# Order of work at the head, at chunks' ends and before the experts in a fused attention and MoE kernel

## The chip, the core and the metric

The kernel runs on one core of a Trainium2 chip. TensorE (PE) multiplies matrices; VectorE (DVE), ScalarE (ACT) and GpSimd (POOL) work on tiles in on-chip memory; SyncE (SP) issues most of the transfers (DMAs). The metric is the time of one execution on the device in microseconds (us). Of the kernel before there are three runs and one profiled execution.

## What is computed

```python
scores = (1 / S) * z @ z.T                  # B = 8, S = 2496, z: S x 64
out = (maximum(scores, 0) ** 2) @ v         # v: S x 256
x = (u * out).reshape(B * S, 256)
logits = x @ w_gate                         # 8 experts
# per token: its best expert, weight = softmax(logits)[best] = gate_w
# per expert e: of its tokens the 80 with the largest gate_w
h = maximum(x[tok_idx] @ w1[e], 0)          # 256 -> 1024
result[tok_idx] = gate_w[tok_idx] * (h @ w2[e])   # all other rows are 0
```

All values are 32-bit floats.

## The kernel before

**Precision.** PE multiplies in a reduced 32-bit format. Each operand is split into a high part (a cast to that format) and a low part (the value less the high part), and three products replace one: high by high, high by low and low by high. So z gives `zs` or `zm`, v gives `vt`, and the attention weights `a` give `ah` and `al`. High parts are casts, on ACT mostly; low parts are subtractions on DVE (helper `tt`, L55).

**Tiles.** A chunk is a batch and 512 of its queries: 8 x 5 = 40 chunks (`at(n)`), each with ten pairs of 128-key tiles. For one pair: scores on PE into two PSUM tiles `s` (`begin`, L399); ACT's Relu (L402) and Square (L405) into `a`; the cast to `ah` on ACT (L408) or, in the chunk's own diagonal blocks, on DVE (L413) (all three in `middle`); `al` on DVE (`low`); then the accumulation on PE into two banks `acc` (`attend_half`, L544), in two groups per pair. The scores are symmetric, so most blocks are computed once: DVE transposes `a` (`turn`, L304), SP writes it to DRAM (`y`) and reads it back as `blk` (L358), where ACT casts it (`mirrored`, L376) and DVE subtracts.

**Loops.** The first chunk's first five steps run in one lane (`for t in range(HALF)`, HALF = 5). Then two chunks run side by side (`for t in range(HALF, END)`): step t handles the entries e and e + 1, while the pairs e + 3 and e + 4 are prepared. Every fifth step ends a chunk: `chunk_x_first` (DVE, `xf`, L569) multiplies u into accumulator bank 0, `chunk_x_copy` (ACT, L584) copies bank 1, and both banks are free for the next chunk only then. Chunks with an even number end in the middle of a step, those with an odd number at its end. In between stand steps for the next batch (`z_and_v`): a load of 512 columns of z (`load_z`, 256 KB), its split (`prep_zs`, L121 and L55), loads and splits of v (`prep_v`, cast L108, low part L159). The last chunk runs in one lane again, beside the logits of the chunk before it (`chunk_logits`, PE L684, from the parts `xb` that `chunk_hi` and `chunk_lo` make).

**What sets the order.** PE, ACT, DVE and SP work in the order in which the program is written (a manual schedule), each engine in its own queue; semaphores hold an instruction until what it reads is there. POOL does the same in the last stage. SP has up to eight DMAs under way: a further one is issued when an older one, whose semaphore it uses again, has landed.

**Head.** A tile `idle` is set to zero on POOL (L181); nine matmuls on it (`warm`, L186) run until z has arrived. Then come the scores of the first two pairs, the whole of v's first tile, and the third pair's scores ahead of the first accumulation. Between the first accumulating matmuls two more `warm` stand.

**Experts.** Behind the attention the experts' tokens are found (`token`, on DVE), their rows are gathered from DRAM by POOL (`xg`, L1589), copied (`xf`, L110), turned by PE (`ffn_x`, `xp`, L1621) and put through two layers (`ffn1`, `ffn2`). The last chunk's gate values are made by DVE (`gate_near`, `gate_sum`: L744 to `gall`, L758), turned by PE (`gt`, L769), copied (`gs`) and written to DRAM (`gate_store`, `gd`, L772), from where `target` gathers them. SP loads the experts' weights (`wraw`, L861).

## Time and profile before

| | us |
|---|---|
| runs before | 1351.98, 1353.8, 1354.32 (median 1353.8) |
| profiled execution, in all | 1355.23 |
| its span, first to last instruction | 1353.3 |
| PE busy | 1329.6 (98%) |
| DVE busy | 1085.8 (80%) |
| ACT busy | 1020.1 (75%) |
| POOL busy | 40.1 (3%) |

The mean granted clock of PE in the profiled execution is 0.993 of full speed. PE's matmuls on 64 rows come in twos that run at the same time in two halves of the array, so "a pair of matmuls" is two rows of the trace. In a timeline a bracket shows how long an engine sat idle before an instruction and who released it. In the list of waits each row has the waiting engine and its tile and line, the one waited for, the sum in us, how many times, and the longest.

### The profile page before, as it was taken

How to read it: one execution, taken by the hardware profiler on the slowest of the kernel's cores; microseconds unless marked ns; L12 is line 12 of the kernel's file. 1: busy time of each engine (PE TensorE's matmuls, PEld its weight loads, DVE VectorE, ACT ScalarE, POOL GpSimd, SP SyncE). 2: the span in 40 equal slices, each digit the busy share in tenths (PEclk: the TensorE clock that was granted, in tenths of full speed). 3: DMA queues.
4: the chain of work that ended last, by engine and by line, in shares of the span. 5: the costliest groups of instructions: out<-in, count | busy, mean ns of one | idle time of the engine just before them, and what ended most of it. 6: DMA issues, size and time to landing. Idle time of an engine off the chain costs nothing.

```text
span 1353.3 us, 32346 instructions
## 1 busy us (share of the span) xinstructions
PE 1329.6 (98%) x12887; PEld 1210.7 (89%) x12887; DVE 1085.8 (80%) x1667; ACT 1020.1 (75%) x1361; POOL 40.1 (3%) x42
## 2 busy tenths in 40 slices
PE   8999999999999999999999999999999999999997
PEld 5789998999899997999889998999889998898776
DVE  6777888887887888878878888878888778777886
ACT  6776787677867787776877778776877678777666
POOL 0000000000000000000000000000000000000065
PEclk8999999999999999999999999999999999999999
DMA  5799989999899998999899998999979997989945
GB/s 164 223 269 258 283 224 289 241 277 244 259 239 250 290 262 227 270 247 261 222 262 269 257 285 225 260 264 261 249 237 243 286 267 214 290 226 274 272 136 188
DMA packets 286013, 337.12 MB, mean 249 GB/s; under 512 B 96824, under 2 KB 206368, under 8 KB 275616
## 3 DMA queue, kind: packets, MB, share of 16 engines
q1 hardware_dynamic: 284832, 333.68, 93.8%
q8 instruction: 103, 1.69, 0.5%
q0 software_dynamic: 1024, 1.31, 0.3%
q14 instruction: 54, 0.44, 0.1%
HBM read 162.67 MB, written 135.48 MB: 220 GB/s over the span
## 4 chain that ended last, share of the span: by engine, by line
PE 83%; DVE 6%; ACT 4%; DMA 4%; issue 2%; SPq 0%; POOL 0%; DVEq 0%; POOLq 0%; ACTq 0%
PE acc L544 69%; PE s L399 9%; PE pl L684 2%; ACT a L402 1%; ACT a L405 1%; DVE al L55 1%; DMA blk<-y 1%; PE s L461 1%; DMA wraw<-w 1%; DVE x L304 1%; DVE vt L159 1%; PE warm L186 0%; ACT xf L584 0%; DMA y<-x 0%; PE op L1699 0%
## 5 line engine op out<-in xcount | busy, mean ns | idle before, releaser
L544 PE MATMUL acc<-ah,vt 64*128 64x512 f32 (+1 forms) x6004 | 845.9, 387 | 6.3 <-DVE xf L569 3.7
L544 PEld LDWEIGHTS acc<-ah,vt 64*128 64x128 f32 x6004 | 660.0, 185 | 60.1 <-DVE xf L569 6.7
L544 PE MATMUL acc<-al,vt 64*128 64x512 f32 (+1 forms) x3002 | 503.9, 389 | 0.4 <-DVE al L55 0.2
L55 DVE TENSOR_TENSOR al<-a,ah 128x1024 fp32r<-128x1024 f32 (+2 forms) x240 | 272.3, 1135 | 174.4 <-ACT ah L408 76.7
L544 PEld LDWEIGHTS acc<-al,vt 64*128 64x128 f32 x3002 | 340.0, 185 | 23.5 <-DVE al L55 1.1
L402 ACT ACTIVATE a<-s 128x512 f32<-128x512 f32 (+1 forms) x408 | 221.0, 594 | 141.7 <-PE s L399 138.8
L376 ACT CAST ah<-blk 128x1024 fp32r<-128x1024 f32 x160 | 167.1, 1047 | 102.7 <-PE acc L544 94.2
L55 DVE TENSOR_TENSOR al<-blk,ah 128x1024 fp32r<-128x1024 f32 x160 | 193.4, 1214 | 38.2 <-PE acc L544 10.7
L405 ACT ACTIVATE a<-a 128x1024 f32<-128x1024 f32 x204 | 216.3, 1060 | 6.3
L304 DVE STREAM_TRANSPOSE x<-a 128x512 f32<-128x512 f32 x320 | 207.6, 687 | 0.0
L408 ACT CAST ah<-a 128x1024 fp32r<-128x1024 f32 x160 | 168.0, 1050 | 5.8 <-PE acc L544 0.8
L399 PE MATMUL s<-zm,zs 64*128 64x512 f32 x960 | 148.7, 392 | 4.1 <-ACT a L402 4.1
L399 PEld LDWEIGHTS s<-zm,zs 64*128 64x128 f32 x960 | 107.2, 185 | 14.3 <-ACT a L402 5.7
L1589 POOL DMA_INDIRECT xg<-xs,tok x8 | 13.0, 1630 | 1294.7 <-ACT w2h L888 1286.1
L159 DVE TENSOR_TENSOR vt<-vraw,vt 128x1024 fp32r<-128x1024 f32 (+1 forms) x40 | 46.3, 1156 | 1.6 <-ACT vt L108 1.3
L55 DVE TENSOR_TENSOR xf<-xf,xb 128x1024 f32<-128x1024 f32 (+1 forms) x38 | 45.2, 1189 | 0.4
L55 DVE TENSOR_TENSOR xb<-xf,xb 128x1024 bf16<-128x1024 f32 (+1 forms) x38 | 45.1, 1186 | 0.2
L108 ACT CAST vt<-vraw 128x1024 fp32r<-128x1024 f32 (+3 forms) x56 | 44.9, 830 | 0.0
L594 ACT CAST xb<-xf 128x1024 bf16<-128x1024 f32 (+1 forms) x39 | 39.8, 1020 | 5.0 <-DVE xf L55 2.8
L602 ACT CAST xb<-xf 128x1024 bf16<-128x1024 f32 (+1 forms) x38 | 38.8, 1020 | 5.4 <-DVE xf L55 5.4
L399 PE MATMUL s<-zm 64*128 64x512 f32 x264 | 42.3, 400 | 0.4 <-ACT a L402 0.4
L413 DVE CAST ah<-a 128x1024 fp32r<-128x1024 f32 (+1 forms) x44 | 29.7, 675 | 14.1 <-ACT a L405 14.1
(190 smaller groups left out, 905.9 us busy)
## 6 DMA issues: line engine op xcount, KB each, us to landing
y<-x SPq DMA_DIRECT2D x80, 1024.0 KB, 6.9
blk<-y SPq DMA_DIRECT2D x320, 256.0 KB, 6.9
out<-idle SPq DMA_DIRECT2D x40, 512.0 KB, 7.8
vraw<-v SPq DMA_DIRECT2D x32, 512.0 KB, 9.3
zm<-zs SPq DMA_DIRECT2D x128, 128.0 KB, 4.8
ut<-uT SPq DMA_DIRECT2D x32, 512.0 KB, 6.8
xs<-xq SPq DMA_DIRECT2D x32, 512.0 KB, 6.6
wraw<-w SPq DMA_DIRECT2D x28, 512.0 KB, 5.3
```

The source lines that it names most:

```text
L55: V.tensor_tensor(out=o, in0=a, in1=b, op=op)
L108: eng.copy(out=o, in_=i)
L159: e1.tensor_tensor(out=vt[:, :nf, 1], in0=raw[:, :nf], in1=vt[:, :nf, 0], op=ALU.subtract)
L304: V.transpose(out=x[:, :, :, t].rearrange("p n k s -> p k n s"), in_=a)
L376: nc.scalar.copy(out=natural(ah), in_=src)
L399: nc.tensor.matmul(s, zk, zm[rows, :, y].rearrange("p h k t -> p k h t"), start=i == 0, stop=i == 2)
L402: nc.scalar.activation(out=a[:, h, :nc_], in_=s[:, :nc_], func=AF.Relu)
L405: nc.scalar.activation(out=a[:, :, :nc_], in_=a[:, :, :nc_], func=AF.Square)
L408: nc.scalar.copy(out=st["ah"][:, :, :nq], in_=a[:, :, :nq])
L544: ins = nc.tensor.matmul(acc[c], vt, mv, start=p == pairs[0] and group == 0 and i == 0, stop=p == pairs[-1] and group == 1 and i == len(mm ...
L594: nc.scalar.copy(out=xb[:, 0], in_=xf)
L602: nc.scalar.copy(out=xb[:, 1], in_=xr)
```

## The change

The kernel after does the same arithmetic on the same tiles; it issues it in another order, splits the first pair's work between two engines, and loads less of z.

- **Head.** The first 128 columns of `idle` are set first and eight warm matmuls read these. `first_pair` computes the first pair's `a` in two halves, one on ACT and one on DVE, with v's first tile loaded and cast in halves between them. The third pair's scores (`begin(2)`) go between the accumulating matmuls, in the place of two warm ones.
- **Single-lane steps.** `middle` loses the cast to `ah`, which becomes a step of its own, `cast`; v's cast stands ahead of it.
- **First two-lane step.** `group(e, 0)` goes ahead of `begin(e + 3)`.
- **Sides of z.** Apart from columns 0 to 511, only those rows and columns are loaded that `zs` uses: two DMAs of 64 KB in pieces of 512 bytes replace one of 256 KB, and two operations on 128 rows replace four on 64.
- **Chunks' ends.** At even ends `chunk_x_first` and `chunk_x_copy` go ahead of `low(e + 3)`; at odd ends ahead of `cast(e + 4)`.
- **z and v.** In `z_and_v` v's split goes ahead of z's.
- **Late steps.** The store and the high and low parts of the chunk before the last are written one entry earlier; a gather into a small unused tile is added on POOL.
- **Experts.** A memset and an empty instruction on POOL stand ahead of the first gather and take its waits for stored rows. The gate values of the last chunk (`gate_near`, `gate_sum`, `gate_store`) go behind the tokens of experts 2 and 3; SP's write of them (`gd`) stands ahead of four weight loads in SP's order, before and after. The sums over counts are spread between the first experts' steps.

```diff
+        if j:
+            raw = raw[:, :CH // 2]
+            load_sides(raw, b, j, j + 1)
+        else:
+            nc.sync.dma_start(out=raw, in_=zT[b, :, :CH])
         return raw
+
+    def load_sides(raw, b, j0, j1):
+
+        for h in range(2):
+            rows = slice(h * HP, (h + 1) * HP)
+            src = zT[b, rows, j0 * CH:j1 * CH].rearrange("p (k h t) -> p k h t", h=2, t=P)
+            nc.sync.dma_start(out=raw[rows].rearrange("p (k t) -> p k t", t=P), in_=src[:, :, h])
...
-        for h in range(2):
-            rows = slice(h * HP, (h + 1) * HP)
-            src = tiles_of(raw)[rows, :, h]
-            V.tensor_copy(out=zs[rows, 0], in_=src)
-            tt(zs[rows, 1], src, zs[rows, 0], ALU.subtract)
+        src = raw.rearrange("p (k t) -> p k t", t=P)
+        V.tensor_copy(out=zs[:, 0], in_=src)
+        tt(zs[:, 1], src, zs[:, 0], ALU.subtract)
...
+            nc.tensor.matmul(wm, idle[:, :P], idle[:, :P].rearrange("p (o t) -> p o t", o=1).broadcast_to([P, QT, P]),
+                             start=True, stop=True)
+
+    warm(8, ps_m, "m")
+    nc.gpsimd.memset(idle[:, P:], 0.0)
...
+    def first_pair(v_high, v_low):
+
+        zm = zm_t[0, 0]
+        a = pair_tile("a", 0, 0, 0, F32, 2)
+        ah = pair_tile("ah", 0, 0, 0, bufs=4)
+        ss = [ps_s.tile([P, CH], F32, tag="s", name=f"s_0_0_{h}") for h in range(2)]
+        for i, (x, y) in enumerate(((0, 0), (1, 0), (0, 1))):
+            for h, s in enumerate(ss):
+                rows = slice(h * HP, (h + 1) * HP)
+                nc.tensor.matmul(s, zm[rows, h, x, 0], zm[rows, :, y].rearrange("p h k t -> p k h t"),
+                                 start=i == 0, stop=i == 2)
+        nc.scalar.activation(out=a[:, 0], in_=ss[0], func=AF.Relu)
+        ts(a[:, 1], ss[1], 0.0, ALU.max)
+        v_high(0)
+        nc.scalar.activation(out=a[:, 0], in_=a[:, 0], func=AF.Square)
+        tt(a[:, 1], a[:, 1], a[:, 1], ALU.mult)
+        nc.scalar.copy(out=ah[:, 0], in_=a[:, 0])
+        V.tensor_copy(out=ah[:, 1], in_=a[:, 1])
+        v_low(0)
+        al = pair_tile("al", 0, 0, 0)
+        tt(al, a, ah, ALU.subtract)
+        a_t[0, 0, 0] = (ah, al)
...
-            if start_up and i == len(ks):
-                warm(2, ps_m, "m")
+            if start_up and i == 2 * len(ks):
+                between()
...
+            vb = b if tm < NP else b + 1
+            if 0 < vb < B and tm in V_SPLIT:
+                g = V_SPLIT[tm]
+                prep_v(vb, g, v_raw.pop((vb, g)), nc.scalar, V)
             if 0 < zb < B:
                 if tm in Z_SPLIT:
                     j = Z_SPLIT[tm]
                     (prep_zs if j else prep_zm)(zb, j, z_raw.pop((zb, j)))
...
         for t in range(HALF):
-            if t == 0:
-                begin(2)
-            group(t, 0)
+            group(t, 0, lambda: begin(2))
             if t:
                 begin(t + 2)
             middle(t + 2)
             first_parts(t)
+            cast(t + 2)
             group(t, 1)
             low(t + 2)
             turn(t + 2)
...
             n_end = t // HALF - 1 if t % HALF == HALF - 1 else None
+            if t == HALF:
+                group(e, 0)
             begin(e + 3)
             middle(e + 3)
-            group(e, 0)
+            cast(e + 3)
+            if t > HALF:
+                group(e, 0)
             finish(t, 0)
             transfers(e)
             group(e + 1, 0)
@@ -1199,18 +1255,22 @@
             if t % HALF == 0:
                 logits(t // HALF - 3, 2)
             group(e, 1)
-            low(e + 3)
             if n_end is not None and n_end % 2 == 0:
                 chunk_x_first(*at(n_end))
                 chunk_x_copy(*at(n_end))
+            low(e + 3)
             turn(e + 3)
             middle(e + 4)
+            second = n_end is not None and n_end % 2 == 1
+            if not second:
+                cast(e + 4)
             finish(t, 1)
             transfers(e + 1)
             group(e + 1, 1)
-            if n_end is not None and n_end % 2 == 1:
+            if second:
                 chunk_x_first(*at(n_end))
                 chunk_x_copy(*at(n_end))
+                cast(e + 4)
             low(e + 4)
...
+                    x = 2 * (i - e) + j
+                    if x == 1:
+                        chunk_store(*at(n))
+                    elif x != NP - 2:
+                        finished(*at(n), x)
+                    if x == 2:
+                        chunk_hi(*at(n))
+                    elif x == NP - 3:
+                        chunk_lo(*at(n))
+                    if x:
+                        finished(*at(n - 1), NP + x)
...
+            xg_t[0] = rows_tile(0)
+            late["stored"].append(nc.gpsimd.memset(xg_t[0][:num(0)], 0))
+            ready = nc.gpsimd.engine_nop()
+            for x in late["stored"]:
+                after(ready, x)
...
             many_pe()
+            many_counts()
+            whole(0)
+            many_products()
+            ffn_x(0)
+            many_fetch((2,))
+            ffn_xl(0)
+            many_rows()
+            many_within()
+            ffn1(0, 0)
+            whole(1)
+            token(2)
+            token(3)
+            ffn_x(1)
             gate_near(B - 1, NQ - 1)
             gate_sum(B - 1, NQ - 1, NQ)
-            whole(0)
-            gate_store(P, NCOL - P, ps_t, "t")
-            ffn_x(0)
-            many_counts()
-            many_fetch((2,))
-            ffn_xl(0)
-            ffn1(0, 0)
-            whole(1)
-            many_rows()
-            many_within()
-            token(2)
-            ffn_x(1)
             ffn_xl(1)
             ffn1(0, 1)
-            token(3)
-            loads(4, PL)
             ffn_h(0, 0)
+            gate_store(P, NCOL - P, ps_t, "t")
+            loads(4, xg_t[3][3])
             many_fetch((4, 6))
             ffn1(1, 0)
             empty()
+            token(4)
             target(0)
             target(1)
-            token(4)
             ffn_h(0, 1)
             whole(2)
             ffn1(1, 1)
             ffn2(0, FIRST_J)
             ffn_x(2)
+            spread(3)
             ffn_xl(2)
             ffn2(0, LAST_J)
             token(5)
@@ -1835,7 +1920,6 @@
             half_lo()
             target(2)
             target(3)
-            spread(3)
```

**ACT at the head.** `a_0_0` is the first pair's weights, `s_` its scores, `vt_0` v's first tile. Before:

```order
L402 ACT_TABLE_LOAD
L402 ACTIVATE a_0_0_154<-s_0_0_155 128x512
L402 ACTIVATE a_0_0_154<-s_0_1_156 128x512
L405 ACTIVATE a_0_0_154<-a_0_0_154 128x1024
L108 CAST vt_0_170<-vraw_0_115 128x4x256
L402 ACTIVATE a_0_2_173<-s_0_2_174 128x512
L402 ACTIVATE a_0_2_173<-s_0_3_175 128x512
L405 ACTIVATE a_0_2_173<-a_0_2_173 128x1024
L402 ACTIVATE a_0_4_206<-s_0_4_207 128x512
L402 ACTIVATE a_0_4_206<-s_0_5_208 128x512
```

After:

```order
L456 ACT_TABLE_LOAD
L456 ACTIVATE a_0_0_156<-s_0_0_158 128x512
L1109 CAST vt_0_149<-vraw_0_116 128x2x256
L459 ACTIVATE a_0_0_156<-a_0_0_156 128x512
L461 CAST ah_0_0_157<-a_0_0_156 128x512
L416 ACTIVATE a_0_2_176<-s_0_2_177 128x512
L416 ACTIVATE a_0_2_176<-s_0_3_178 128x512
L1109 CAST vt_0_149<-vraw_0_116 128x2x256
L419 ACTIVATE a_0_2_176<-a_0_2_176 128x1024
L416 ACTIVATE a_0_4_221<-s_0_4_222 128x512
```

The cast of v's first tile is two halves now, the second behind the next pair's relus, and the first pair's cast to `ah` (on DVE before) stands in part on ACT.

**DVE at the first even chunk's end.** `xf_0` reads accumulator bank 0; `zs_1` is the next batch's z. Before:

```order
L121 CAST zs_1_843<-zraw_585 64x256
L55 TENSOR_TENSOR zs_1_843<-zraw_585,zs_1_843 64x256
L121 CAST zs_1_843<-zraw_585 64x256
L55 TENSOR_TENSOR zs_1_843<-zraw_585,zs_1_843 64x256
L475 CAST ah_1_6_860<-a_1_6_848 128x512
L55 TENSOR_TENSOR al_1_6_897<-a_1_6_848,ah_1_6_860 128x512
L55 TENSOR_TENSOR al_1_6_897<-shared,ah_1_6_860 128x512
L569 SCALAR_TENSOR_TENSOR xf_0_900<-acc_0_0_217,ut_0_602 128x512
L55 TENSOR_TENSOR al_2_2_918<-blk_2_0_649,ah_2_2_904 128x1024
```

After:

```order
L130 CAST zs_1_841<-zraw_581 128x256
L55 TENSOR_TENSOR zs_1_841<-zraw_581,zs_1_841 128x256
L610 SCALAR_TENSOR_TENSOR xf_0_892<-acc_0_0_211,ut_0_599 128x512
L516 CAST ah_1_6_856<-a_1_6_844 128x512
L55 TENSOR_TENSOR al_1_6_897<-a_1_6_844,ah_1_6_856 128x512
L55 TENSOR_TENSOR al_1_6_897<-shared,ah_1_6_856 128x512
L55 TENSOR_TENSOR al_2_2_914<-blk_2_0_646,ah_2_2_900 128x1024
```

`xf` stands right behind z's split, which has two operations instead of four, and ahead of `ah` and the two low parts.

**DVE at the first experts.** `xf` is an expert's gathered rows, `tok` its tokens' numbers, `gall` the last chunk's gate values. Before:

```order
L744 TENSOR_SCALAR fw_4_19253,nsum<-d_4_19249 128x32
L746 SCALAR_TENSOR_TENSOR ex_4_19251<-ex_4_19251,fw_4_19253 128x32
L55 TENSOR_TENSOR s_7_4_19407<-ex_4_19251 128x16
L55 TENSOR_TENSOR s_7_4_19409<-s_7_4_19407 128x8
L55 TENSOR_TENSOR s_7_4_19411<-s_7_4_19409 128x4
L59 TENSOR_SCALAR s_7_4_19411<-s_7_4_19411 128x4
L758 RECIPROCAL gall<-s_7_4_19411 128x4
L110 COPY xf_19415<-xg_19344 80x2x256
L771 COPY gs_19419<-gt_19417 32x128
L1516 TENSOR_REDUCE cnt_all<-scratch 128x6
L55 TENSOR_TENSOR xTl_19433<-xp_19422,xTh_19425 128x160
L110 COPY xf_19444<-xg_19359 80x2x256
```

After:

```order
L121 COPY xf_19405<-xg_19331 80x2x256
L1666 TENSOR_SCALAR lw_19407,j_19408<-ws_19389,rin_all 80x256
L61 TENSOR_SCALAR tok_19410<-j_19408,base_all 80x1
L1666 TENSOR_SCALAR lw_19414,j_19415<-ws_19389,rin_all 80x256
L61 TENSOR_SCALAR tok_19417<-j_19415,base_all 80x1
L784 TENSOR_SCALAR fw_4_19223,nsum<-d_4_19219 128x32
L786 SCALAR_TENSOR_TENSOR ex_4_19221<-ex_4_19221,fw_4_19223 128x32
L55 TENSOR_TENSOR s_7_4_19428<-ex_4_19221 128x16
L55 TENSOR_TENSOR s_7_4_19430<-s_7_4_19428 128x8
L55 TENSOR_TENSOR s_7_4_19432<-s_7_4_19430 128x4
L59 TENSOR_SCALAR s_7_4_19432<-s_7_4_19432 128x4
L798 RECIPROCAL gall<-s_7_4_19432 128x4
```

The chain from `fw` to `gall` stood ahead of the first `xf`; it begins behind the second `xf` and two tokens now.

## Rows read from the trace of the kernel before

**Rows 1.** the page: busy time by engine, the DMA queue, the chain by engine
```profile
PE 1329.6 (98%) x12887; PEld 1210.7 (89%) x12887; DVE 1085.8 (80%) x1667; ACT 1020.1 (75%) x1361; POOL 40.1 (3%) x42
...
q1 hardware_dynamic: 284832, 333.68, 93.8%
...
PE 83%; DVE 6%; ACT 4%; DMA 4%; issue 2%; SPq 0%; POOL 0%; DVEq 0%; POOLq 0%; ACTq 0%
```

**Rows 2.** PE's waits, whole run: who waited for whom, us in total, times, longest
```profile
PE s L399 <- ACT a L402: 4.5, 5, 2.0
PE acc L544 <- DVE xf L569: 3.7, 5, 1.5
...
PE xp L1621 <- DVE xf L110: 1.4, 2, 0.7
PE acc L544 <- DVE vt L159: 1.3, 4, 0.4
PE pl L684 <- DVE xb L55: 1.1, 1, 1.1
```

**Rows 3.** timeline of the first 17 us: start, us, what xcount [idle before <-releaser]
```profile
1.39 4.02 PE L186 MATMUL warm<-idle 128*128 128x512 bf16 x9 [1.39 <-POOL idle L181]
...
7.03 1.08 ACT L402 ACTIVATE a<-s 128x512 f32<-128x512 f32 x2 [4.93 <-PE s L399]
...
7.68 0.96 PE L399 MATMUL s<-zm 64*128 64x512 f32 x5 [0.42 <-ACT a L402]
...
9.11 1.03 ACT L108 CAST vt<-vraw 128x1024 fp32r<-128x1024 f32 x1
...
10.68 1.65 PE L399 MATMUL s<-zm,zs 64*128 64x512 f32 x5 [2.03 <-ACT a L402]
...
11.71 1.48 PE L544 MATMUL acc<-ah,vt 64*128 64x512 f32 x4
```

**Rows 4.** two stretches after that: us, busy (xcount) by engine, PEclk, DMA share, GB/s
```profile
11.70:17.20 5.50, 5.37 (x21) 2.78 (x19) 4.67 (x8) 4.53 (x6) 0.00 (x0) 0.50 0.58 164
17.20:29.00 11.80, 11.80 (x102) 9.47 (x100) 7.25 (x12) 8.19 (x11) 0.00 (x0) 1.00 0.37 130
```

**Rows 5.** the chain of waits, 42 to 51 us: start, us, what
```profile
42.49 7.88 DMA blk<-y
...
50.43 0.04 ACT ah L376
```

**Rows 6.** timeline at the first step of two lanes
```profile
34.72 0.29 DVE L121 CAST zs<-raw 64x256 fp32r<-64x256 f32 x1
35.05 0.42 DVE L55 TENSOR_TENSOR zs<-raw,zs 64x256 fp32r<-64x256 f32 x1
...
35.74 0.96 PE L399 MATMUL s<-zm,zs 64*128 64x512 f32 x5 [1.37 <-ACT a L402]
```

**Rows 7.** timeline at an even and at an odd chunk's end
```profile
70.70 0.68 DVE L569 SCALAR_TENSOR_TENSOR xf<-acc,ut 128x512 f32<-128x512 f32 x1
...
71.43 0.95 PE L544 MATMUL acc<-ah,vt 64*128 64x512 f32 x5 [1.46 <-DVE xf L569]
...
227.62 1.05 ACT L408 CAST ah<-a 128x1024 fp32r<-128x1024 f32 x1
...
228.57 0.59 ACT L584 ACTIVATE xf<-acc 128x512 f32<-128x512 f32 x1
```

**Rows 8.** timeline at the first experts
```profile
1291.53 0.42 DVE L110 COPY xf<-xg 80x512 uint16<-80x512 uint16 x1
...
1291.67 0.29 PE L769 MATMUL gt<-ident,gall 128*32 128x128 f32 x1 [0.56 <-DVE gall L758]
```

**Rows 9.** DMA issues: KB each, median us to landing; and SP's own waits
```profile
zraw<-zT SPq DMA_DIRECT2D x36, 256.0 KB, 7.5
...
shared<-yd SPq DMA_DIRECT2D x144, 64.0 KB, 5.1
...
SPq L358 <- DMA blk<-y: 19.3, 24, 1.2
```

More of the change, by code (lines that the diff above doesn't have):

```diff
@@ L426, in scores @@
         on_v = k // QT == qc
-        return square, low, turn
+        return square, cast, low, turn
+    def first_pair(v_high, v_low):
[19 more added lines that the diff above has]
+        a_t[0, 0, 0] = (ah, al)
     def two_parts(x):
@@ L484, in low @@
                 folded.add((b, qc, k))
-        return square, low, None
+        return square, cast, low, None
     acc_t = {}
@@ L847, in raw_part, with load_raw @@
         return raw.rearrange("p (c f) -> p c f", c=n // 2), src[:, part * n // 2:(part + 1) * n // 2]
-    def load_raw(e, which, part, after=None):
+    def load_raw(e, which, part, behind=None):
         pool, tag = keep, "vraw"
@@ L876, in attn_moe_kernel, with loads @@
     pieces, ready = [], []
-    def loads(n, after=None):
+    def loads(n, behind=None):
         n = min(n, NR - len(ready) - len(halves))
         for p in pieces[:n]:
-            ready.append((p, load_raw(*p, after)))
+            ready.append((p, load_raw(*p, behind)))
         del pieces[:n]
@@ L1066, in attn_moe_kernel, with v_high, v_low @@
     if True:
+        v_t[0, 0] = vpool.tile([P, QT, 2, D], F32R, tag="vt", name="vt_0_0")
+        def v_high(h):
+            nc.scalar.copy(out=v_t[0, 0][:, 2 * h:2 * h + 2, 0], in_=vraw0[:, 2 * h:2 * h + 2])
+        def v_low(h):
+            vt = v_t[0, 0][:, 2 * h:2 * h + 2]
+            tt(vt[:, :, 1], vraw0[:, 2 * h:2 * h + 2], vt[:, :, 0], ALU.subtract)
         prep_zm(0, 0, raw0)
         prep_zs(0, 1, raw12[:, 0])
-        first = scores(0, 0, 0)
-        first[0]()
-        first[1]()
-        prep_v(0, 0, vraw0, nc.scalar, V)
-        first = scores(0, 0, 2)
-        first[0]()
-        first[1]()
+        first_pair(v_high, v_low)
+        second_pair = scores(0, 0, 2)
+        v_high(1)
+        second_pair[0]()
+        v_low(1)
+        second_pair[1]()
+        second_pair[2]()
         v_raw[0, 1] = vraw1
@@ L1110, in whole @@
             middle(i)
+            cast(i)
             low(i)
```

109 lines of the change are left out of this document (57 added, 52 removed).

## The prediction

> **What bounds the kernel now.** I read the page first, then the waits of TensorE (PE), then the timeline at each wait the change touches. PE is busy 1329.6 of 1353.3 us and carries 83% of the chain that ended last; VectorE (DVE) and ScalarE (ACT) have a fifth and a quarter of the span free, and the hardware DMA queue is at 93.8% [rows 1]. So a saving on DVE or ACT counts only where PE waits for it. The groups of waits that matter here are few: for scores behind a relu 4.5 us, for a chunk's last multiplication (xf) 3.7, for the first experts' rows 1.4, for v's low half 1.3, for the late logits 1.1 [rows 2]. Beside them stands one loss that is no wait: between 11.7 and 17.2 us the granted clock is 0.50, and 21 matmuls take what 102 take in 11.8 us afterwards (0.26 against 0.12 us each) [rows 4]. About 15 us are within reach in all; the rest of the span is matmuls that the change leaves as they are.
>
> **The head and the first steps.** Before, the warm matmuls start at 1.39, when the idle tile is set, and nine of them end at 5.41, 0.45 apart; the first relu starts at 7.03, 1.6 after them [rows 3]. Then ACT does two relus (1.08), a square and the whole v cast (1.03) and the next relus; PE waits 2.03 us for these and reaches the first accumulating matmul at 11.71 [rows 3]. After: a quarter of the idle tile is set first and eight matmuls are issued; with one fewer (0.45) and some 0.3 from the shorter fill, warming ends near 4.7 and the first relu starts near 6.3. ACT then has four operations of half a tile (relu, v, square, cast), each some 0.54 by the pair of relus [rows 3], while DVE does the other half: 6.3 + 2.2 = 8.5 for the first accumulating matmul, 3.2 us ahead. From there to the end of the first pair PE has 12 pairs of accumulating matmuls and the three score pairs that are moved in between them. At full clock a pair takes 11.80 / 102 x 2 = 0.23 us [rows 4], so 15 x 0.23 = 3.5 and the end is at 12.0, against 17.2: 5.2 us gained. At half clock a pair takes 0.45, so 6.7 and the end is at 15.2: 2.0 gained.
>
> Which clock it will be the trace of before only bounds. There the scores run at the full pace of 0.23 a pair from 7.68, right behind a wait of 0.42, and the clock fell only around the wait of 2.03 [rows 3]. The waits left in the new order are by the sum above 0.6 (scores behind the first relu) and about 0.5 (before the accumulating matmuls); they are nearer to the 0.42 that did no harm than to 2.03. I take full clock, and keep half clock as a rival, since the two filling warm matmuls at 13.1 go. The Trainium skill speaks against this part: its page "TensorE: Matmul & The Clock Gate", section "Part 1: The HAM clock gate (the "warmup" mystery)", has the array's clock gated by how busy PE has lately been. By it, an idle stretch without filling matmuls may keep the lower rate, and the head would gain 2.0 instead of 5.2; the trace agrees in so far as 0.50 is granted behind the wait of 2.03.
>
> What comes next in line is not PE. At 50.43 ACT casts the first mirrored block in the moment that its DMA lands, 7.88 us after the last issue [rows 5]; PE takes that block at once. The issue stands behind DVE's work in SP's order. PE would come to this block earlier than it can land, by the head's gain and by the waits of 0.44 (29.5 us), 1.37 (35.7) and 0.42 (40.1) that the earlier v cast and the group ahead of the scores take away (the 1.37 is in [rows 6]). So those 2.2 us are not added: the gain at 50 us is that of DVE's chain, which is the head's plus what DVE no longer does. Splitting one chunk of z takes half the instructions, 0.29 + 0.42 = 0.71 us less [rows 6], and two such splits stand ahead of the block: 1.4. At full clock this makes up to 6.6, at half clock up to 3.4; I take **5.0**, since v's first half must land by 6.8 and the block's landing may not move by as much; bounds 2.0 and 6.6.
>
> **The loop, 40 to 1240 us.** At an even chunk's end xf (0.68, from 70.70) stands behind the low parts of the pair after next, and PE waits 1.46 for it [rows 7]; five such waits sum to 3.7 [rows 2]. The change puts xf ahead of a cast and two subtractions of together 1.8 us, which is more than each wait: **3.7** gone. The low parts come 0.68 later, and are covered by the group that PE still has ahead of them, some 2.8 us (12 x 0.23); without that cover they would cost 0.68 each. At an odd end xf's copy (0.59) follows the cast of ah (1.05) on ACT [rows 7]; PE's matmuls stand 0.1 to 0.15 us there and restart at half pace, at ten of the ends, some 0.27 us over the usual spacing. Bounds 1.0 (the idle time alone) and 2.7; I take **1.8**, the middle, because no row shows a restart by itself. V ahead of z: of the four waits for v's low half (1.3) one lies in the first 40 us; the other three are 0.30 each, behind 1.4 us of z work that now comes later: **0.9**. z's sides take about 23 us of work from DVE in all (32 x 0.71), on the path nowhere else in the loop: 0. On SP each of the loop's 28 loads becomes two issues, some 0.4 us more each, and half of the bytes; that is hidden while SP is ahead (a rival below).
>
> **The late steps.** The last chunk's low part is written one step earlier: the wait of 1.1 for it [rows 2] goes, **1.0**. The extra gather there is on GpSimd, which does nothing else then: 0.
>
> **The first experts.** The gates' chain on DVE (fw to gall, 1.5 us) goes behind the tokens, so that the first rows are copied (1291.53 [rows 8]) some 0.8 earlier, and the second and third gathers are issued ahead of the four weight loads instead of among them; the waits for rows at experts 2 and 3 (1.4 [rows 2]) should go. Against that, gall, for which PE waits 0.56 at 1291.67 [rows 8], now comes near 1296.4, and PE would stand there some 0.7. Working it through, the second experts' first layer begins 0.4 later than before, the third's 1.3 earlier. I take **1.0**; bounds -0.5 and 2.0. The weight loads that are pushed back by some 5 us are used from 1312 on, and landed by 1301 before: covered, with 6 us left; without that cover each microsecond counts.
>
> **Sum.** 5.0 + 3.7 + 1.8 + 0.9 + 1.0 + 1.0 = 13.4. The profiled execution took 1355.23 (its span 1353.3), 1.4 above the median of 1353.8: 1355.2 - 13.4 - 1.4 = 1340.4.
>
> **Rivals.** First, the clock stays at half through the head: 2.0 to 3.4 instead of 5.0, so 1342.0 to 1343.4. For it speaks that PE idles twice without filling, against it that both gaps are small. Second, the waits at the chunks' ends only move: what xf passes (ah, the low parts) is late in its turn, the loop gives 2.0 instead of 6.4, and the time is 1344.8; with the first rival, 1347.5. For it: DVE and ACT at three quarters and more; against: 2.8 us of matmuls as cover. Third, slower: SP's ring. SP already waits 19.3 us in 24 places for an older DMA before it can issue a block's next part, up to 1.2 each [rows 9]. Each z load becomes two DMAs of 64 KB, and the second takes one more place in that ring. If a block behind it comes late by 0.4 for the issue and 1.2 for the place, 1.6 us, PE loses this each time the block has no slack. It decides from about 8 of the 28 loads on (13.4 / 1.6); at 12 the time is 1340.4 + 19 = 1359. Against it: in the loop ACT's waits for a block's landing are next to none after that first one, and the nearest row of 64 KB lands in 5.1 against 7.5 for z's 256 KB [rows 9]. The Trainium skill, page "DMA: Bandwidth & Descriptors", section "Bandwidth", advises large DMAs and calls those under 64 KB bound by their descriptors; these loads arrive at that border. By that rule the halved bytes would save no queue time. Fourth, the change doesn't do what it says, because the order written is overruled by a wait of the same engine: 1353.8. The order shows the instructions moved, so this is small.
>
> **How the numbers follow.** Forecast as summed 0.60; clock low 0.18; waits move 0.11 (with both, 0.03 of it); ring 0.05; nothing 0.06. The likeliest is the first, 1340.4. The range runs from all upper bounds, 6.6 + 3.7 + 2.7 + 0.9 + 1.1 + 2.0 = 17.0 (1336.8) and a little for restarts at the even ends, so 1335, up to the first two rivals together, 1348; outside are the ring and the case of nothing. A measurement of this kernel tells 0.2% (2.7 us) from no change: faster 0.90, same 0.05, slower 0.05.
>
> **What would show it.** In the profile after: the first accumulating matmul near 8.5 and a PEclk of 1.00 from 8.5 on (half clock: 0.50 up to 15); ACT's cast of the first mirrored block near 45 and still released by a DMA; no wait for xf at L610 or for vt in the loop; the late logits without a wait; PE waiting for gall near the second expert, and none for the third's rows. I am wrong if the head's gain is gone by 60 us, if PE's waits in the loop have new names of the same sum, or if SP's wait for blocks grows by tens of microseconds and ACT's idle time is ended by them.

## The result and the profile after

Five runs of the changed kernel took 1311.3 to 1313.82 us, median 1312.5, against 1353.95 for five runs of the kernel before: a ratio of 0.9697, 95% interval 0.9683 to 0.971. Faster, as forecast, but by 41 us instead of 13.4, and outside the range of 1335 to 1348. The profiled execution took 1313.82 (its span 1312.1, against 1353.3).

The page of the kernel after (busy time by engine; the DMA queue; the chain by engine) answers to [rows 1]:

```profile
PE 1296.7 (99%) x12884; PEld 1248.5 (95%) x12884; DVE 1062.3 (81%) x1606; ACT 1017.3 (78%) x1362; POOL 38.4 (3%) x45
...
q1 hardware_dynamic: 289568, 329.49, 94.2%
...
PE 92%; DVE 2%; ACT 2%; DMA 2%; issue 1%; POOL 0%; SPq 0%; POOLq 0%; ACTq 0%; DVEq 0%
```

PE's busy time itself fell by 33 us, for all but the same matmuls. PE's waits and SP's own (total, times, longest) answer to [rows 2] and [rows 9]:

```profile
PE pl L725 <- DVE xb L55: 1.8, 1, 1.8
...
PE s L413 <- ACT a L416: 0.9, 3, 0.4
...
PE gt L809 <- DVE gall L798: 0.6, 1, 0.6
...
SPq L372 <- DMA blk<-y: 19.7, 24, 1.1
```

The waits for xf, for vt and for the experts' rows are gone; the one for the late logits is 1.8 in place of 1.1. The head, in the timeline (start, us, what) and in the windows (us, busy and count by engine, PEclk, DMA share, GB/s), against [rows 3] and [rows 4]:

```profile
1.08 3.59 PE L195 MATMUL warm<-idle 128*128 128x512 bf16 x8 [1.08 <-POOL idle L190]
...
6.29 0.60 ACT L456 ACTIVATE a<-s 128x512 f32<-128x512 f32 x1 [4.18 <-PE s L454]
...
7.07 1.64 PE L413 MATMUL s<-zm 64*128 64x512 f32 x5 [0.39 <-DVE a L59]
...
8.62 2.06 PE L585 MATMUL acc<-ah,vt 64*128 64x512 f32 x8
```

```profile
11.70:17.20 5.50, 5.37 (x48) 4.35 (x48) 4.53 (x7) 5.22 (x8) 0.00 (x0) 1.00 0.74 201
17.20:29.00 11.80, 11.80 (x106) 9.49 (x104) 10.18 (x16) 11.51 (x15) 0.00 (x0) 1.00 0.50 174
```

The first accumulating matmul starts at 8.62 (forecast 8.5), but not at the full clock. The eight matmuls there take 2.06 us, and their pairs start 0.43 apart, as the pairs of before do where 0.50 was granted; from 10.5 on they start 0.23 apart. (The trace's first record of the clock, 1.00, stands at 10.54 here. Ahead of it PEclk reads 1.00 only because there is no record.) This belongs to the execution and not to the kernel: in eleven of the thirteen profiled executions with this head, experiments below included, the first record, 1.00, stands at 4.4 to 6.6. In c_gate, one of them, the same eight matmuls take 1.19, behind a wait of 0.60, and the next scores start 0.85 earlier than in after:

```profile
8.62 1.19 PE L585 MATMUL acc<-ah,vt 64*128 64x512 f32 x8 [0.60 <-ACT ah L461]
9.65 0.85 PE L413 MATMUL s<-zm,zs 64*128 64x512 f32 x6
```

The first mirrored block is cast 7.1 us earlier than in [rows 5], still in the moment that its DMA lands:

```profile
43.37 1.05 ACT L390 CAST ah<-blk 128x1024 fp32r<-128x1024 f32 x1 [3.65 <-DMA blk<-y]
```

**Where the time came from.** DVE's xf marks a chunk's end. Its rows for the second chunk and for the chunk before the last but one, of before and then of after:

```profile
102.98 0.68 DVE L569 SCALAR_TENSOR_TENSOR xf<-acc,ut 128x512 f32<-128x512 f32 x1
...
1237.51 0.68 DVE L569 SCALAR_TENSOR_TENSOR xf<-acc,ut 128x512 f32<-128x512 f32 x1
```

```profile
93.07 0.69 DVE L610 SCALAR_TENSOR_TENSOR xf<-acc,ut 128x512 f32<-128x512 f32 x1
...
1195.93 0.68 DVE L610 SCALAR_TENSOR_TENSOR xf<-acc,ut 128x512 f32<-128x512 f32 x1
```

So 9.9 us were gained up to the first mark, 31.7 in the loop between the marks (1134.5 to 1102.9), and behind it 0.4 were lost (115.8 to 116.2). The forecast had 5.0, 6.4 (of which the first even end's 1.5 lies ahead of the first mark) and 2.0. The loop holds the surprise: between the marks PE's waits were 3.1 us in the list and some 1.2 at the odd ends, each too short for the list, and 32 were gained. A stretch of undisturbed matmuls shows why, of before and then of after:

```profile
72.24 0.84 PE L544 MATMUL acc<-al,vt 64*128 64x512 f32 x4
72.71 1.30 PE L544 MATMUL acc<-ah,vt 64*128 64x512 f32 x8
73.64 0.85 PE L544 MATMUL acc<-al,vt 64*128 64x512 f32 x4
```

```profile
60.23 0.84 PE L585 MATMUL acc<-al,vt 64*128 64x512 f32 x4
60.68 1.29 PE L585 MATMUL acc<-ah,vt 64*128 64x512 f32 x8
61.59 1.06 PE L413 MATMUL s<-zm,zs 64*128 64x512 f32 x6
```

Eight matmuls, four pairs, take 0.93 us from start to start before and 0.91 after; both at a granted clock of 1.00. Over the starts of all pairs of 512 columns from 100 to 1200 us the mean is 232.5 ns before and 227.7 after: before, most lie scattered between 228 and 241; after, 84% are at 228 or below. The groups by shape give their number in after (half of 4912 + 2456, so 3684 pairs):

```profile
L585 PE MATMUL acc<-ah,vt 64*128 64x512 f32 x4912 | 695.2, 387 | 0.4 <-DVE ah L429 0.4
L585 PE MATMUL acc<-al,vt 64*128 64x512 f32 x2456 | 418.9, 389 | 0.3
```

At 4.8 ns each these are 17.7 us. Another 819 pairs have 448 columns and came only 1 ns closer. Nothing in the change's words touches a single matmul's pace.

### The profile page after: what moved, and what is told of

The parts are those of the page before. It is cut to its first block, busy times and chain, and to the rows that moved or that the text cites. A ratio compares the mean times of both kernels' runs of the same rounds, so it can differ in the third digit from the quotient of the medians.

```text
span 1312.1 us, 32286 instructions
## 1 busy us (share of the span) xinstructions
PE 1296.7 (99%) x12884; PEld 1248.5 (95%) x12884; DVE 1062.3 (81%) x1606; ACT 1017.3 (78%) x1362; POOL 38.4 (3%) x45
## 3 DMA queue, kind: packets, MB, share of 16 engines
q1 hardware_dynamic: 289568, 329.49, 94.2%
## 4 chain that ended last, share of the span: by engine, by line
PE 92%; DVE 2%; ACT 2%; DMA 2%; issue 1%; POOL 0%; SPq 0%; POOLq 0%; ACTq 0%; DVEq 0%
PE acc L585 76%; PE s L413 10%; PE pl L725 2%; DMA wraw<-w 1%; PE s L500 1%; PE acc L556 1%; DMA wall<-w 1%; PE op L1783 0%; ACT a L416 0%; DVE w1l L935 0%; PE warm L195 0%; ACT a L419 0%; DVE w2l L935 0%; PE hp L1742 0%; DVE al L55 0%
## 5 line engine op out<-in xcount | busy, mean ns | idle before, releaser
L585 PE MATMUL acc<-ah,vt 64*128 64x512 f32 (+1 forms) x6004 | 831.5, 383 | 0.4 <-DVE ah L429 0.4
L585 PEld LDWEIGHTS acc<-ah,vt 64*128 64x128 f32 x6004 | 683.4, 184 | 10.3 <-DVE ah L429 0.8
L585 PEld LDWEIGHTS acc<-al,vt 64*128 64x128 f32 x3002 | 349.4, 184 | 5.7 <-DVE al L55 0.9
L416 ACT ACTIVATE a<-s 128x512 f32<-128x512 f32 x406 | 220.3, 595 | 109.5 <-PE s L413 104.4
L413 PEld LDWEIGHTS s<-zm,zs 64*128 64x128 f32 x960 | 111.9, 184 | 4.6 <-ACT a L416 2.2
L610 DVE SCALAR_TENSOR_TENSOR xf<-acc,ut 128x512 f32<-128x512 f32 (+3 forms) x44 | 28.2, 649 | 20.8 <-PE acc L585 20.4
L625 ACT ACTIVATE xf<-acc 128x512 f32<-128x512 f32 (+1 forms) x38 | 22.4, 589 | 28.6 <-PE acc L585 24.1
```

The costliest lines, as they stand in the source:

```text
L413: nc.tensor.matmul(s, zk, zm[rows, :, y].rearrange("p h k t -> p k h t"), start=i == 0, stop=i == 2)
L416: nc.scalar.activation(out=a[:, h, :nc_], in_=s[:, :nc_], func=AF.Relu)
L585: ins = nc.tensor.matmul(acc[c], vt, mv, start=p == pairs[0] and group == 0 and i == 0, stop=p == pairs[-1] and group == 1 and i == len(mm ...
```

## Experiments: the pace of the matmuls

Two places of the diff, not among the lines shown further up, had been taken for nothing. They make a small tile its own (128 bytes more per partition in the pool `gp`) and take another from the constants (64 bytes less):

```diff
-    wg_r = const.tile([P, DC, E], F32, name="wg_r")
+        wg_r = gp.tile([P, NT, E], F32, tag="d", name="wg_r")[:, :DC]
...
-                o = gp.tile([P, NT, E // 2], F32, tag="s4", name=f"lg2_{b}_{qc}")
-                o = o.rearrange("p t e -> p (t e)")[:, :QT * E].rearrange("p (t e) -> p t e", e=E)
+                o = gp.tile([P, QT, E], F32, tag="lg2", name=f"lg2_{b}_{qc}")
```

By this the tiles behind move: the accumulations' weights `vt` start at byte 28608 of a partition before and at 28544 after, the moving operand `ah` at 186176 and 186240. So the distance, `ah` less `vt`, leaves a rest of 128 when divided by 256 (128 modulo 256) before, and 0 after. The other buffers of both, and `al`, leave the same rest. Ten kernels differ in this; the pace is the mean of the starts as above:

| kernel | order of work | (ah - vt) mod 256 | pace, ns | median, us | ratio to before |
|---|---|---|---|---|---|
| before | before | 128 | 232.5 | 1353.95 | |
| b_pad64 | before | 128 | 232.4 | 1353.05 | 0.9994 [0.9984, 1.0004] |
| b_main64 | before | 192 | 233.4 | 1354.68 | 1.0007 [0.9998, 1.0017] |
| b_vt64 | before | 192 | 233.4 | 1355.05 | 1.0006 [0.9996, 1.0015] |
| b_order | before | 0 | 228.1 | 1338.23 | 0.9895 [0.9878, 0.9911] |
| b_lay | before | 0 | 227.9 | 1336.87 | 0.9885 [0.9868, 0.9901] |
| a_all64 | after | 128 | 233.2 | 1335.71 | 0.986 [0.9844, 0.9877] |
| a_main64 | after | 64 | 230.5 | 1323.36 | 0.9779 [0.9763, 0.9795] |
| after | after | 0 | 227.7 | 1312.5 | 0.9697 [0.9683, 0.971] |
| a_rel256 | after | 0 | 227.7 | 1313.47 | 0.9708 [0.9692, 0.9724] |

**All tiles 64 bytes on (b_pad64).** Before, with an unused constant, which puts `vt` on a multiple of 256 and leaves all distances.

```diff
+    const.tile([P, 16], F32, name="pad")
```

> The kernel before, with one unused tile of 64 bytes per partition behind idle in the constants, so that every later tile starts 64 bytes higher; no instruction differs. Theory A (where the operands start sets the pace of PE's matmuls: before, ah, al, zs and vt all start 64 bytes past a multiple of 128, after, all on one): pairs of 512 columns at 0.2267 us instead of 0.2327, some 5500 pairs, so about 33 us less: 1321, and PE's waits as before (16 us). Theory B (the pace follows from the waits that the reordering took away): 1354, pairs at 0.2327.

1353.05 us at the old pace: moving every later tile by 64 bytes does nothing by itself.

**The new order in the old places (a_all64).** After, with the same constant and `lg2` back in its old tile.

```diff
+    const.tile([P, 16], F32, name="pad")
...
-                o = gp.tile([P, QT, E], F32, tag="lg2", name=f"lg2_{b}_{qc}")
+                o = gp.tile([P, NT, E // 2], F32, tag="s4", name=f"lg2_{b}_{qc}")
...
```

> The kernel after, with such a tile of 64 bytes, and the logits' second half in the tile that it had before (128 bytes less, to make room): vt, ah, al and zs start where they did before, 64 bytes past a multiple of 128. Theory A: pairs at 0.2327 again, 1312.5 + 33 = about 1345, though PE's waits stay gone. Theory B: 1312, pairs at 0.2267.

1335.71: in the old places all of the reordering is worth 18.2 us against before, and the places another 23.2.

**Later pools moved by 64 bytes in before (b_main64), and vt's pool too (b_vt64).** Now the moving operands, or `vt`, start on multiples of 128, and the distance is 192.

```diff
     main = ExitStack()
+    padp = main.enter_context(tc.tile_pool(name="padp", bufs=1))
+    padp.tile([P, 16], F32, name="pad2")
```

> The kernel before with 64 bytes ahead of the later pools alone: the moving operands (ah, al, zs) start on a multiple of 128, the weights (vt, zm) 64 past one as before. Theory A with the moving operand as its cause: all of the gain, about 1321. With the weights as its cause: 1354. If both matter: between. Theory B: 1354.

> The kernel before with the weights (vt, zm) on a multiple of 128 and the moving operands (ah, al, zs) 64 past one. Theory A with the moving operand as its cause: 1354. With the weights as its cause: about 1321. Theory B: 1354.

Both stay at before's time, at a pace within 1 ns of before's. Neither operand's own place is the cause.

**The distance alone, by another way (b_order).** Before, with `vpool` created behind `gp`, not a byte added.

```diff
-    vpool = weights.enter_context(tc.tile_pool(name="vpool", bufs=NV))
...
     gp = weights.enter_context(tc.tile_pool(name="gp", bufs=1))
+    vpool = weights.enter_context(tc.tile_pool(name="vpool", bufs=NV))
```

> The kernel before with the pool of vt created behind the pool of small gate tiles: no instruction differs, every hot tile still starts 64 bytes past a multiple of 128 or 256, but the moving operand (ah, al) now starts a multiple of 2048 bytes from the weights (vt), as in the kernel after, instead of 128 bytes short of one. Theory C (the distance of moving operand and weights sets the pace): pairs at 0.2267 us instead of 0.2327, 5500 x 6 ns = 33 us less, about 1321, with PE's waits as before. Theory B (the pace follows from the waits that the reordering took away): 1354.

1338.23, 15.7 less, with every instruction in its old place in the order. Of the pools that are in use in the loop `vpool` alone changes its place modulo 256 here.

**The change's two tile lines alone (b_lay).** Before with the diff at the head of this section.

> The kernel before with two edits of the change alone: the second half of the late logits in a tile of its own (128 bytes), and wg_r in a gate tile instead of a constant. Nothing is reordered; the distance of ah and vt becomes a multiple of 2048. Theory C: about 1321. Theory B: 1354.

1336.87, 17 us less than before; by the marks 14.5 of it lie in the loop, 1120.0 between them instead of 1134.5. (The rest can't be read from the two traces: before's lost some 4 us more to the clock in the head, as shown below.) The windows (us, PE busy and count, PEld, DVE, ACT, POOL, PEclk, DMA, GB/s) of before, then of b_lay:

```profile
100.00:1200.00 1100.00, 1095.67 (x11134) 1018.58 (x11132) 892.93 (x1319) 840.20 (x1111) 0.00 (x0) 1.00 0.99 256
```

```profile
100.00:1200.00 1100.00, 1093.72 (x11296) 1024.68 (x11294) 899.12 (x1332) 852.05 (x1128) 0.00 (x0) 1.00 0.99 259
```

In the same 1100 us PE is busy 2 us less and gets through 162 recorded matmuls more. Its waits didn't shrink. Those at the odd ends, 0.1 to 0.15 us each and some 1.2 in all before, grew to 2.3, since PE comes to them earlier now:

```profile
PE acc L544 <- DVE xf L569: 3.9, 5, 1.6
PE acc L544 <- ACT xf L584: 2.3, 10, 0.3
```

**The period (a_rel256) and a step between (a_main64).** After, with 256 bytes of small gate tiles put ahead of `vt` (a distance 256 less); and after with b_main64's padding.

```diff
     weights = ExitStack()
+    gq = weights.enter_context(tc.tile_pool(name="gq", bufs=1))
...
-                o = gp.tile([P, QT, E], F32, tag="lg2", name=f"lg2_{b}_{qc}")
+                o = gq.tile([P, QT, E], F32, tag="lg2", name=f"lg2_{b}_{qc}")
...
```

> The kernel after with 256 bytes of small gate tiles moved ahead of vt's pool: ah starts 256 bytes short of a multiple of 2048 from vt, all starts stay on multiples of 128. Theory C with a period of 256 bytes or less: 1312, pairs at 0.2267. With a longer period: pairs at about 0.233 and 1345. Theory B: 1312.

> The kernel after with 64 bytes ahead of the later pools: ah and al 64 bytes past a multiple of 2048 from vt, and zs 64 past one from zm. Theory C: pairs at about 0.233 (as in the two kernels of before with 64 bytes off), 1312 + 33 = 1345. Theory B: 1312.

At 256 the pace is that of after; at 64 it lies in the middle, 230.5. The padding of a_main64 also moves `zm` against `zs`, so its 10.9 us may not be `ah` and `vt` alone. By size: a_all64 takes 1123.7 between the marks (94.15 to 1217.90), 20.8 more than after. The starts of the accumulating pairs of 512 columns there, 3395 in number, give 18.0 of these (5.3 ns each); those of the pairs of 448 columns give 1.7 and those of the scores 1.8, and the logits' matmuls take back 0.6.

## Experiments: the parts of the order

Each undoes one part of the kernel after, which keeps its places and its pace (227.6 to 227.8 in all of them). A difference between two kernels is known to 2 or 3 us.

**The chunks' ends (c_ends), the even ones alone (c_even), the odd ones alone (c_odd).**

```diff
             group(e, 1)
+            low(e + 3)
             if n_end is not None and n_end % 2 == 0:
                 chunk_x_first(*at(n_end))
                 chunk_x_copy(*at(n_end))
-            low(e + 3)
...
-            if not second:
-                cast(e + 4)
+            cast(e + 4)
...
-                cast(e + 4)
```

> The kernel after with the chunks' ends alone as before (x behind the low parts at even ends, behind the cast at odd ones). Theory 1 (the ends cost what PE waits there): in the run with the two tile edits alone PE waits 3.9 us at even and 2.3 at odd ends, so 1312.5 + 6.2 = 1318.7. Theory 2 (a wait also costs a slower pace of the pairs behind it): more, 1321 to 1325, with pairs of 0.231 us behind the waits. By the forecast's own terms (3.7 and 1.8): 1318.0.

> The kernel after with the even chunks' ends alone as before (x behind the low parts). PE waits 3.1 us in five places there when both kinds of ends are as before. Theory 1 (an end costs its wait): 1315.6. Theory 2 (each end costs more than its wait, evenly spread over the twelve microseconds that both kinds cost together): 1312.5 + 12.2 x 3.1 / 5.4 = 1319.5.

> The kernel after with the odd ends alone as before (x's copy behind the cast of ah). PE waits 2.3 us in ten places there. Theory 1: 1314.8. Theory 2: 1317.7. Theory 3 (a cost per stop, not per microsecond: fifteen stops cost 12.2 us, so 0.8 each): 1320.5 here, and 1316.5 with the even ends alone as before.

1324.74 (0.9782 [0.9763, 0.98]), 1318.65 (0.974 [0.9723, 0.9757]) and 1318.95 (0.9741 [0.9725, 0.9758]): 12.2, 6.1 and 6.4 us more than after, though PE's waits that return are 5.4, 3.2 and 2.3. One even stop of c_even and one odd stop of c_odd show what a wait leaves out (timeline of PE):

```profile
61.27 0.39 PE L585 MATMUL acc<-ah,vt 64*128 64x512 f32 x1
62.45 1.19 PE L585 MATMUL acc<-ah,vt 64*128 64x512 f32 x7 [0.79 <-DVE xf L610]
63.25 0.62 PE L585 MATMUL acc<-al,vt 64*128 64x512 f32 x3
```

```profile
215.73 0.39 PE L585 MATMUL acc<-ah,vt 64*128 64x512 f32 x1
216.34 1.19 PE L585 MATMUL acc<-ah,vt 64*128 64x512 f32 x7 [0.22 <-ACT xf L625]
217.14 0.85 PE L585 MATMUL acc<-al,vt 64*128 64x512 f32 x4
```

Eight matmuls take 0.91 undisturbed. Here they take 63.25 - 61.27 = 1.98 and 217.14 - 215.73 = 1.41: 1.07 for a wait of 0.79, 0.50 for one of 0.22. Each stop costs 0.28 beyond its wait: the profile counts idle time from the end of the last matmul, 0.39 after its start, where the next pair would have started 0.23 after it, and of one pair a matmul started ahead of the wait (x1), so that its twin runs alone behind it. They restart at the full pace (seven in 0.80). So five even stops are 3.2 + 1.4 = 4.6, and ten odd ones 2.3 + 2.8 = 5.1, together 9.7 of the 12.2 measured. Between the marks c_even takes 4.3 more than after, which is four even stops at 1.07, c_odd 6.8, which is 1.8 more than ten odd stops at 0.50, and c_ends 11.0. So the rest stands at the odd ends; what it is stays open.

**The head (c_head).** The first pair, the warm matmuls and v's first tile as before.

```diff
...
-        first_pair(v_high, v_low)
...
+        first = scores(0, 0, 0)
...
-            group(t, 0, lambda: begin(2))
+            if t == 0:
+                begin(2)
+            group(t, 0)
```

> The kernel after with the first pair as before: whole tiles on ACT, nine warm matmuls and two more, the third pair's scores ahead. By the forecast's term for the head and first steps 5.0 us: 1317.5; by the two traces' distance at the second chunk's end, which the run with the tile edits alone reaches 5.1 us after the kernel after: 1317.6. If the gain comes from the later steps' order instead: under 1315.

1316.99 (0.9726 [0.9703, 0.9749]): 4.5 more. The wait of 2.03 returns. Its five runs lie between 1314.8 and 1320.21, further apart than after's, and in the profiled one the granted clock is 0.50 from 10.74 to 14.15, so part of the 4.5 is the clock.

**Its clock.** Runs with the head of before don't agree on it. These are 11.7 to 17.2 us of b_pad64 and of b_vt64:

```profile
11.70:17.20 5.50, 5.37 (x44) 3.88 (x44) 4.65 (x8) 4.04 (x6) 0.00 (x0) 1.00 0.71 189
```

```profile
11.70:17.20 5.50, 5.37 (x25) 2.76 (x23) 4.66 (x9) 4.14 (x6) 0.00 (x0) 0.58 0.62 183
```

PE waits 2.02 to 2.03 us ahead of both. In four profiled executions with before's head (b_pad64, b_main64, b_order, b_lay) the clock stayed at 1.00, in three (before, b_vt64, c_head) it fell for some microseconds. In the four the first record of 1.00 stands at 4.6 to 5.8 us, in the three at 6.0 to 7.3. The first xf stands at 70.7 in before and at 66.3 to 66.7 in the four: some 4 us of [rows 4] belong to that execution and not to the kernel.

**z's sides and z behind v (c_z).** z loaded whole, four operations, ahead of v's split.

```diff
-            load_sides(raw, b, j, j + 1)
+        nc.sync.dma_start(out=raw, in_=zT[b, :, j * CH:(j + 1) * CH])
...
-        V.tensor_copy(out=zs[:, 0], in_=src)
-        tt(zs[:, 1], src, zs[:, 0], ALU.subtract)
...
+            for h in range(2):
+                rows = slice(h * HP, (h + 1) * HP)
+                src = tiles_of(raw)[rows, :, h]
+                V.tensor_copy(out=zs[rows, 0], in_=src)
+                tt(zs[rows, 1], src, zs[rows, 0], ALU.subtract)
...
```

> The kernel after with z loaded whole and split in four operations again in all batches but the first, and z ahead of v there. By the forecast 0.9 us for v's waits: 1313.4. Rival (DVE's 0.7 us of work for each of 28 loads reach PE, or halved bytes relieve the DMA queue): 1316 or more, with new waits of PE for DVE or for blocks.

1316.47 (0.9721 [0.9703, 0.974]): 4.0 more by the medians, 2.4 by the spans (1314.5 and 1312.1). Its first xf is 0.9 later (61.9 against 61.0; 60.6 in c_gate, whose head like c_z's had the full clock), and the waits for v return, three stops:

```profile
PE acc L588 <- DVE vt L171: 1.0, 3, 0.3
```

With 0.28 for each stop these are 1.8, and between the marks c_z takes 1.5 more than after (1104.4); 0.9 + 1.8 = 2.7, or 3.1 by c_gate, lies in what was measured.

**The single-lane cast (c_cast) and the first two-lane group (c_group).**

```diff
-            first_parts(t)
             cast(t + 2)
+            first_parts(t)
...
-            if t == HALF:
-                group(e, 0)
...
-            if t > HALF:
-                group(e, 0)
+            group(e, 0)
```

> The kernel after, with v's cast again behind the cast to ah in the first five steps. The forecast's theory: what comes next in line at 50 us is the first mirrored block, so a wait that returns ahead of it (0.44 us at the half-cast v) costs nothing beyond the head's gain: 1312.5 to 1312.8. Rival, the sums of the other runs: about 2.6 us of the gain stand in the parts not undone so far, and this is one of them: 1313.3 to 1314, with a wait of PE for vt of 0.4 us or more near 22 us.

> The kernel after, with the first two-lane step's scores again ahead of a group. The forecast's theory: the wait of 1.37 us for the scores' buffers returns at about 29 us but the first mirrored block ends later anyway, so nothing: 1312.5 to 1312.8. Rival: PE pays the wait and a restart in full, 1314.3 (1.37 and 0.4 to 0.6).

c_cast: 1315.64 (0.9719 [0.9705, 0.9732]), 3.1 more by the medians, 0.6 by the spans (1312.7 and 1312.1), so the size is open: after's profiled execution is the slowest of its five and c_cast's the fastest. c_group: 1313.16 (0.9694 [0.9681, 0.9707]), no difference, although its wait is back; its first xf stands at 60.55, and at 60.56 in c_gate, which has after's order there. The scores' waits of c_group, then the first mirrored block on ACT in c_group, in c_cast and in b_lay:

```profile
PE s L413 <- ACT a L416: 2.2, 3, 1.5
```

```profile
42.88 1.05 ACT L390 CAST ah<-blk 128x1024 fp32r<-128x1024 f32 x1 [4.02 <-DMA blk<-y]
```

```profile
44.06 1.05 ACT L390 CAST ah<-blk 128x1024 fp32r<-128x1024 f32 x1 [3.81 <-DMA blk<-y]
```

```profile
46.02 1.05 ACT L376 CAST ah<-blk 128x1024 fp32r<-128x1024 f32 x1 [3.58 <-DMA blk<-y]
```

A stop of 1.5 us ahead of that block costs nothing when the block comes no later. The cast order, which holds up the chain to the block, moves it by 0.7 against after's 43.37, and by 1.2 against the 42.88 of c_group, which like c_cast had the full clock in the head.

**The experts (c_gate).** Experts, gate values and gathers in before's order.

```diff
...
+            gate_near(B - 1, NQ - 1)
+            gate_sum(B - 1, NQ - 1, NQ)
+            whole(0)
+            gate_store(P, NCOL - P, ps_t, "t")
...
```

> The kernel after with the order of the gates and the first experts as before. By the forecast 1.0 us slower: 1313.5. By the traces, whose last stretch from the last chunk but two on takes 115.8 us before and 116.2 after, no slower or 0.4 faster: 1312.

1313.64 (0.9701 [0.9683, 0.9719]): 1.1 more by the medians and 0.3 behind the last mark (116.5 for 116.2), which can't be told from nothing; the waits for the experts' rows return, with 1.3 us.

**The late steps: as before (c_late), and one step earlier still (d_late).**

```diff
-                    if x == 1:
-                        chunk_store(*at(n))
...
+                    finished(*at(n), 2 * (i - e) + j)
...
```

```diff
             chunk_mid(b, qc)
+            chunk_lo(b, qc)
         elif r == 3:
-            chunk_lo(b, qc)
             chunk_store2(b, qc)
```

> The kernel after, with the store and the high and low parts of the chunk before the last at their old entries. The forecast gave 1.0 us to this part: 1313.5, with the wait of 1.1 us for the late logits' low part back and the present one of 1.8 us gone or smaller. Rival, the reading of the milestones (no gain behind chunk 37): the wait only changes its name, 1312.2 to 1312.8.

> The kernel after with one edit of its own: the last low part of the last chunk but one is written one late step earlier, behind its middle part, so that DVE makes it before the step's weights and blocks. In the kernel after PE waits 1.8 us for it. If that wait alone goes: 1312.5 - 1.8 = 1310.7. If DVE's own queue makes the next blocks late instead: 1312.5.

1312.97 (0.9696 [0.9682, 0.971]) and 1312.53 (0.9693 [0.9677, 0.9709]): no difference either way. Behind the last mark PE's longest wait in d_late, to be set beside the 1.8 of after, is:

```profile
PE pl L663 <- DVE xf L610: 1.1, 1, 1.1
```

The wait for the logits' low part is gone, a new one of 1.1 for DVE's xf stands there, and the stretch behind the last mark is no shorter (116.5 for 116.2). No experiment was faster than after by more than the runs scatter.

## Why the prediction was right in direction and wrong in size

By the medians: places 17.0 (b_lay), ends 12.2, head 4.5, z and v 4.0, cast 3.1, experts 1.1, and 0.7 and 0.5 for the group and the late steps, 43.1 for 41.4 measured. By the ratios, each taken against runs of before in its own round, they are 15.6, 11.5, 3.9, 3.2, 3.0, 0.5, and -0.4 and -0.1, together 37 of 41.0; so the parts of 4 us and less are uncertain in size. Between the marks, where the head and its clock don't enter, places give 20.8 (a_all64), ends 11.0 and z and v 1.5, 33.3 for 31.7. The parts are not quite additive: the reordering gives 18.2 in the old places (a_all64) and 24.4 in the new (b_lay to after), the places 17.0 with the old order and 23.2 with the new.

- **"The rest of the span is matmuls that the change leaves as they are."** This is the step that failed, and with 17 to 23 us by the medians the largest part of the miss of 28. The matmuls are the same instructions, but two tile lines in the diff changed how far apart their operands lie, and so their pace: 227.7 ns for a pair in place of 232.5. The working read the diff for order only, and took the pace of [rows 4] for a constant; rounded to 0.23 us it couldn't show the change. The range left it out as well.
- **Even ends 3.7, odd ends 1.8.** The waits were the right ones and they went; mis-sized was the price of a stop. Measured are 6.1 and 6.4 by the medians of c_even and c_odd. At an even end 0.28 per stop had been left out. At the odd ends the guess of a restart at half pace was wrong in kind: in c_odd they restart at full pace, and each stop costs 0.5 in two spacings, of which the working saw the first. And a PE with a faster pace waits there more, which [rows 2] couldn't show.
- **The head 5.0.** The first accumulating matmul (8.62 for 8.5) and the block's DMA as the limit were right. The full clock from 8.5 on was not, in after's profiled execution, where the head ran at half pace up to 10.5; most executions with this head had it. Undoing the head costs 4.5 by the medians, the clock's fall included at least in the profiled run, so that it is near 5.0 is partly luck. In the profiled pair the first xf came 9.7 and the block 7.1 earlier, more than the upper bound of 6.6: some 4 of these are the clock's fall in that one execution of before, which the sum took for a property of the kernel. With the full clock in both and the same places (b_lay to c_group) the block comes 3.1 earlier, at 42.88 for 46.02. One reading was off: 17.2 is where before's clock rises and not the end of the first pair, of which four of twelve pairs start later, up to 17.95. c_group confirms that a wait ahead of the block isn't to be added; c_cast shows that the cast order is no such wait.
- **z and v 0.9, z's sides 0.** Too low: 2.4 to 4.0. Of it 0.9 to 1.3 stands in the first chunk (the forecast had this under the head), the rest in three stops for v that were given their waits alone.
- **The late steps 1.0.** Wrong: the time behind the last mark didn't shrink. The wait for the low part went to the logits of the next chunk (1.8), as the rival "waits only move" had it for the loop. In the loop that rival was wrong: between 40 and 1200 us after has one listed wait, of 0.3.
- **The experts 1.0.** Neither shown nor refuted: 1.1 by the medians, 0.3 behind the last mark. The waits for rows (1.4) went, but PE waits 0.8 and 0.5 for two other tiles there now (`scratch`, `bt_rest`); in all, PE's listed waits behind the marks are 4.7 us, and were 4.1. PE's wait for gall stayed at 0.6, as forecast (0.7).
- **The ring.** It wasn't seen: SP waits 19.7 us for older blocks, against 19.3 in [rows 9], and the queue's share is 94.2% against 93.8%.
- **The clock.** The rival had it stay low up to 15. In after's profiled execution it stayed low up to 10.5, which cost some 0.9; with before's head its fall comes and goes.

## What to carry to other kernels

Read a diff for where it puts tiles, too: a tile that is added, dropped or given another tag shifts all that lie behind it, and where one engine is always busy, two per cent in the pace of its instructions can outweigh every wait that is left (here 17 to 23 us against some 15). Measure the pace as the distance of starts in undisturbed stretches, before and after, ahead of looking for waits. Here a stop of PE cost its wait and about 0.3 us more. A loss that stands in one profiled execution alone (here the clock's fall) is not yet the kernel's.

## What was not expected of the hardware

Two matmuls on 64 rows that run side by side, with 512 columns in the reduced 32-bit format, start every 227.7 ns when the moving operand and the weights start a multiple of 256 bytes apart in a partition, and every 232 to 233 ns at 128 and 192 modulo 256; at 64 it was 230.5. Three kernels without an instruction moved (b_pad64, b_order, b_lay) show that it is the distance and not the place. The tiles of the later pools move together, so that it is `ah` and `al`, the matmul's own operands, and no other tile of those pools, is the likely reading but not shown. With 448 columns the steps are others: about 203 ns at 0, 201 at 64, 204 at 128 and 202 at 192, so the rule isn't one for all widths. That reads of the two operands get in each other's way would fit, but no run shows this. Distances between these steps, and other kinds of matmuls, were not looked at.
